# A two-branch attention kernel: the hand-built interleaving of its jobs replaced by a list scheduler with modelled engine times

## The chip, the cores and the metric

The kernel runs on one core of one Trainium2 chip. The metric is device time in microseconds (us) of one execution. The kernel before takes 1214.83 us (median of 3 runs, 1211.84 to 1217.28). A core has five engines that each work through their own instruction stream in order: PE (TensorE: matmuls, results go to PSUM), ACT (ScalarE), DVE (VectorE), POOL (GpSimd) and SP (which issues transfers). They wait for one another by semaphores. Both kernels share out eight PSUM tiles of 128 x 512 fp32, called banks below.

## The reference, cut to what matters

```python
x = A_x                                             # 1 x 2048 x 512, bf16
g = sigmoid((x * gate_w).sum(-1, keepdims=True))
# A: full attention, 32 heads of 16
qkv = (x @ A_wqkv) ...
p = softmax(einsum("bhqd,bhkd->bhqk", q, k) * 16 ** -0.5)
a = einsum("bhqk,bhkd->bhqd", p, v) ... @ A_wo
# B: each position looks at 8 earlier ones, 2 apart (same sizes, own weights)
...
return g * a + (1 - g) * b
```

The heavy part is A's exponentials. Scores are made transposed, in tiles of 128 keys x 512 queries of one head: 4 query chunks x 32 heads x 16 key blocks = 2048 tiles. A *period* is one query chunk of four heads: 64 tiles, and there are 32 periods. B runs beside it, mostly on POOL.

## The kernel before

Each tile needs one score matmul (32 rows of the array, 128 columns), one exponential, and one accumulating matmul (128 rows, 17 columns). Most tiles are exponentiated on ACT in sets of three or two, out of two PSUM rings (3 + 2 banks). Exactly six tiles of each period go to DVE instead, which does exp with four operations. One bank is the accumulator, one (`misc`) serves all projections and output jobs, one (`wv`) the DVE exps.

```python
CFG = dict(dve_units=6, burst_budget=2, fill_min=1, pv_lag=2, ...)

def misc_ps(shape, dtype=FP32, tag="misc"):          # ONE bank for all side jobs
    return ps.tile(shape, dtype, tag=tag, bufs=1, name="misc_ps")

def emit_junk():                                     # filler: result never read
    jt = misc_ps([128, QW])
    mm_ct(jt, ident[:], ones_t[:], True, True)       # four matmuls, 128 rows x 32 columns each

def emit_dve(k, u_):                                 # a tile for DVE
    wv = ps.tile([128, QW], FP32, tag="wv", bufs=1, name="wv")
    mm(wv[:], kt_all[...], qt_tiles[(c_, i)][...], True, True, ...)
    dve_ops.extend([ ... four lambdas: ta, ta, ta, pd ... ])

for k in range(nsets + LAG):                         # one step = one exp set
    flush_deadline(k)                                # jobs whose step has come
    ...
    if even:
        emit_qk(k, False)                            # score matmuls + the ACT exp
        cost = pop_misc(k, budget, only_continue=True)
        emit_pv(k - LAG)                             # accumulate set k-2
        cost += pop_misc(k, budget - cost)           # a budget of side work
        if cost < cfg["fill_min"] and k < nsets:
            emit_junk()
    ...
    pop_bg(k, 1)
    pop_dve(2)                                       # two DVE operations per step
```

So the order on every engine is set by counting exp sets, with budgets and deadlines in sets; no engine's time is known to it.

## Time and profile before

| | before |
|---|---|
| time | 1214.83 us |
| ACT busy / PE busy / DVE busy | 877 / 911 / 828 us of 1213.8 |
| exp tiles on ACT / DVE | 1856 / 192 |
| first exp starts at | 30.4 us |
| ACT waits for score matmuls | 277 us |
| mean clock granted to PE | 0.89 |

The page of the kernel before; the rows of digits are busy tenths in 40 equal slices of the span, PEclk is PE's clock in tenths of full speed:

```profile
span 1213.8 us, 22328 instructions
...
PE 911.3 (75%) x9313; PEld 279.6 (23%) x9313; DVE 827.5 (68%) x1306; ACT 877.3 (72%) x763; POOL 590.5 (49%) x540
...
PE   5877677877847676887777787777777877777775
...
ACT  1766666766847677878777777777788878797874
...
PEclk9898998988879888879898988788799998898898
```

No engine is full, and the clock is often not. The costliest groups (count | busy us, mean ns of one | idle us before them and what ended it): ACT's exps, the filler on PE, and the first of the four DVE operations of an exp tile.

```profile
L107 ACT ACTIVATE pT<-ring 128x1536 bf16<-128x1536 f32 x743 | 868.4, 1246 | 301.4 <-PE ring L116 277.2
...
L116 PE MATMUL misc_ps<-ones_t,ident 128*32 128x512 bf16 x1360 | 209.2, 422 | 13.1 <-DVE qt L107 10.1
...
L107 DVE TENSOR_SCALAR ta<-wv 128x512 f32<-128x512 uint16 x192 | 131.4, 684 | 89.8 <-PE wv L116 87.5
```

The waits (total us, times, longest us). ACT, the engine with most work that cannot be avoided, waits 277 us for PE; PE waits 112 us for DVE to free the only `wv` bank:

```profile
engine line waited for: us in total, times, longest us
...
ACT pT L107 <- PE ring L116: 277.2, 190, 14.0
...
PE wv L116 <- DVE pd L107: 111.5, 72, 4.2
```

Between stops ACT is fed well. In this piece of PE's timeline (start, duration) the score matmuls of a set of three start at 608.87 and again at 611.14: five tiles in 2.27 us, ACT's own pace.

```profile
608.87 0.39 PE L116 MATMUL ring<-qt,kt_all 32*128 32x512 bf16 x3 [0.42 <-ACT pT L107]
...
609.20 0.39 PE L116 MATMUL acc<-pT,vp_all 128*17 128x512 bf16 x2
...
610.39 0.39 PE L116 MATMUL ring<-qt,kt_all 32*128 32x512 bf16 x2
611.14 0.39 PE L116 MATMUL ring<-qt,kt_all 32*128 32x512 bf16 x3 [0.36 <-ACT pT L107]
```

The stop itself, as PE's timeline has it, idle time in brackets:

```profile
769.87 0.58 PE L116 MATMUL wv<-qt,kt_all 32*128 32x512 bf16 x1 [3.78 <-DVE pd L107]
```

And windows of 2.5 us around it (busy us and instructions of PE, PE's weight loads, DVE, ACT, POOL; then the clock):

```profile
core 0: us, PE busy (x) PEld busy (x) DVE busy (x) ACT busy (x) POOL busy (x), PEclk, DMA share, GB/s
765.00:767.50 2.50, 1.09 (x16) 0.17 (x9) 2.46 (x3) 1.93 (x3) 2.36 (x2) 1.00 0.00 0
767.50:770.00 2.50, 0.13 (x1) 0.00 (x0) 2.21 (x4) 0.84 (x1) 2.33 (x4) 0.66 0.00 0
770.00:772.50 2.50, 2.50 (x18) 0.67 (x19) 1.94 (x3) 0.00 (x0) 2.50 (x3) 0.50 0.00 0
772.50:775.00 2.50, 2.33 (x16) 0.32 (x11) 1.76 (x4) 2.10 (x2) 2.50 (x3) 0.50 0.30 69
775.00:777.50 2.50, 2.44 (x19) 0.52 (x20) 1.80 (x3) 1.09 (x2) 2.34 (x3) 0.50 1.07 343
777.50:780.00 2.50, 2.50 (x35) 0.73 (x25) 0.58 (x1) 1.74 (x3) 2.50 (x3) 0.80 0.96 331
```

From about 766.1 to 769.9 PE does nothing: it stands at a `wv` matmul until DVE is through. The clock falls within that stop and is 0.50 for some ten microseconds, and ACT starves meanwhile. Such a stop comes about once per period: in the whole trace PE stands idle for over 2 us 28 times, start included, and there are 32 periods.

### The profile page before, as it was taken

How to read it: one execution, taken by the hardware profiler on the slowest of the kernel's cores; microseconds unless marked ns; L12 is line 12 of the kernel's file. 1: busy time of each engine (PE TensorE's matmuls, PEld its weight loads, DVE VectorE, ACT ScalarE, POOL GpSimd, SP SyncE). 2: the span in 40 equal slices, each digit the busy share in tenths (PEclk: the TensorE clock that was granted, in tenths of full speed). 3: DMA queues.
4: the chain of work that ended last, by engine and by line, in shares of the span. 5: the costliest groups of instructions: out<-in, count | busy, mean ns of one | idle time of the engine just before them, and what ended most of it. 6: DMA issues, size and time to landing. Idle time of an engine off the chain costs nothing.

```text
span 1213.8 us, 22328 instructions
## 1 busy us (share of the span) xinstructions
PE 911.3 (75%) x9313; PEld 279.6 (23%) x9313; DVE 827.5 (68%) x1306; ACT 877.3 (72%) x763; POOL 590.5 (49%) x540
## 2 busy tenths in 40 slices
PE   5877677877847676887777787777777877777775
PEld 3323221322212121212122222122222222122221
DVE  4866887787637676667666767666767677766665
ACT  1766666766847677878777777777788878797874
POOL 2014564719193748293929292929475656500000
PEclk9898998988879888879898988788799998898898
DMA  6011102003001132020200202202020021000000
GB/s 206 14 36 49 40 1 87 24 24 119 1 1 40 49 105 70 1 70 1 70 1 1 92 23 79 70 1 70 1 70 1 15 75 35 1 1 1 1 2 18
DMA packets 44397, 47.61 MB, mean 39 GB/s; under 512 B 2260, under 2 KB 41732, under 8 KB 44296
## 3 DMA queue, kind: packets, MB, share of 16 engines
q1 hardware_dynamic: 44296, 46.19, 12.0%
q8 instruction: 72, 1.18, 0.4%
q14 instruction: 29, 0.24, 0.1%
HBM read 39.86 MB, written 6.33 MB: 38 GB/s over the span
## 4 chain that ended last, share of the span: by engine, by line
DVE 41%; PE 31%; ACT 16%; issue 9%; POOL 2%; DMA 0%; ACTq 0%; POOLq 0%; DVEq 0%
DVE ta L107 17%; ACT pT L107 15%; PE misc_ps L116 14%; PE ring L116 7%; PE acc L116 7%; DVE pd L107 5%; PE wv L116 3%; DVE ott L107 2%; DVE qt L107 2%; POOL prod L107 2%; DVE kt_all L107 2%; DVE oat L107 2%; DVE accT L107 2%; DVE kmax_all L107 1%; DVE absq L107 1%
## 5 line engine op out<-in xcount | busy, mean ns | idle before, releaser
L107 ACT ACTIVATE pT<-ring 128x1536 bf16<-128x1536 f32 x743 | 868.4, 1246 | 301.4 <-PE ring L116 277.2
L116 PE MATMUL acc<-pT,vp_all 128*17 128x512 bf16 x1856 | 354.7, 418 | 10.6 <-ACT pT L107 9.9
L116 PE MATMUL ring<-qt,kt_all 32*128 32x512 bf16 x1856 | 293.2, 416 | 54.2 <-ACT pT L107 51.8
L107 POOL TENSOR_TENSOR prod<-vsh,attn 128x512 f32<-128x512 bf16 x128 | 140.0, 1125 | 348.2 <-issue 164.8
L107 DVE SCALAR_TENSOR_TENSOR ta<-ta,wv 128x512 f32<-128x512 f32 x384 | 263.1, 685 | 11.5
L107 POOL TENSOR_TENSOR prod<-prod 128x512 f32<-128x512 f32 x192 | 223.8, 1180 | 5.0
L116 PE MATMUL misc_ps<-ones_t,ident 128*32 128x512 bf16 x1360 | 209.2, 422 | 13.1 <-DVE qt L107 10.1
L107 POOL TENSOR_TENSOR prod<-ksh,qb 128x512 f32<-128x512 bf16 x128 | 146.4, 1175 | 103.9 <-DVE qb L107 96.9
L107 DVE TENSOR_SCALAR ta<-wv 128x512 f32<-128x512 uint16 x192 | 131.4, 684 | 89.8 <-PE wv L116 87.5
L116 PE MATMUL wv<-qt,kt_all 32*128 32x512 bf16 x192 | 81.3, 424 | 111.5 <-DVE pd L107 111.5
L116 PEld LDWEIGHTS <-vp_all 128*17 128x17 bf16 x2048 | 95.6, 92 | 285.1 <-issue 256.2
L107 DVE SCALAR_TENSOR_TENSOR pd<-ta,wv 128x512 uint16<-128x512 f32 x192 | 131.9, 687 | 7.1
L116 PEld LDWEIGHTS <-kt_all 32*128 32x128 bf16 x2048 | 64.6, 92 | 311.2 <-issue 308.9
L116 PE MATMUL misc_ps<-xT,wst 128*16 128x512 bf16 x1024 | 96.2, 437 | 5.2 <-ACT xT L107 3.1
L116 PE MATMUL acc<-pd,vp_all 128*17 128x512 bf16 x192 | 81.6, 425 | 0.6 <-DVE pd L107 0.6
L107 DVE STREAM_TRANSPOSE accT<-acc 128x512 f32<-128x512 f32 x32 | 22.8, 712 | 77.1 <-PE acc L116 77.1
L116 PE MATMUL misc_ps<-bw,xT 128*32 128x512 bf16 x768 | 66.8, 410 | 5.6 <-DVE kvs L107 3.3
L116 PEld LDWEIGHTS <-ident 128*32 128x32 bf16 x1360 | 55.6, 96 | 53.7 <-issue 46.2
L116 PE MATMUL misc_ps<-woarr,oat 128*32 128x512 bf16 x512 | 48.4, 435 | 7.6 <-DVE oat L107 2.6
L116 PEld LDWEIGHTS <-xT 128*32 128x32 bf16 (+1 forms) x1088 | 38.4, 99 | 43.3 <-issue 35.3
L107 DVE CAST kvs<-misc_ps 128x512 bf16<-128x512 f32 x32 | 22.1, 689 | 35.1 <-PE misc_ps L116 35.1
L116 PEld LDWEIGHTS <-wst 128*16 128x16 bf16 x1024 | 32.0, 95 | 49.7 <-issue 37.6
(79 smaller groups left out, 580.3 us busy)
## 6 DMA issues: line engine op xcount, KB each, us to landing
ksh<-kv_scr SPq DMA_DIRECT2D x16, 1024.0 KB, 8.7
vsh<-kv_scr SPq DMA_DIRECT2D x16, 1024.0 KB, 6.3
kv_scr<-kvs SPq DMA_DIRECT2D x16, 256.0 KB, 2.1
out_dram<-osb SPq DMA_DIRECT2D x16, 128.0 KB, 1.7
wst<-in_A_wqkv_dram SPq DMA_DIRECT2D x3, 512.0 KB
bw<-in_B_wqkv_dram SPq DMA_DIRECT2D x1, 1536.0 KB
xld<-in_A_x_dram SPq DMA_DIRECT2D x2, 512.0 KB, 5.7
xld_70<-in_A_x_dram SPq DMA_DIRECT2D x1, 512.0 KB, 7.1
```

Source lines behind the costliest of these rows:

```text
L107: return chain_on(key, f(*a, **k))
L116: return chain(nc.tensor.matmul(out, lhsT=lhsT, rhs=rhs, start=start, stop=stop, **kw))
```

## The change

Nearly everything is rewritten. Each job (a projection, an exp set, a DVE exp, a B block, ...) becomes a generator that yields steps with an engine, a priority and a modelled duration, and takes and gives back buffers by name. A small list scheduler runs all jobs in modelled time while the program is built; the order in which it starts steps becomes the order on each engine. The two single-purpose PSUM banks become one pool of two slots, `w`. Two streams take tiles for DVE whenever a slot is free that no other job wants. The core of the diff:

```diff
-def misc_ps(shape, dtype=FP32, tag="misc"): ...        # and "wv" for DVE exps
-def emit_junk(): ...
-for k in range(nsets + LAG): ...
+class Plan:
+    LAT = 0.08
+    def run(self):
+        while True:
+            # engine step or buffer request that can start earliest in modelled time
+            ...
+            x = min((y for y in lst if y[2] <= st + 1e-9), key=lambda y: (y[0], y[1]))   # priority
+            x[5]()                                      # emits the instructions
+            self.free[nm] = st + x[4]                   # modelled duration
+            self.advance(x[3], st + x[4] + self.LAT, None)
+P.resource("w", 2)
+P.resource("rA", 1); P.resource("rB", 1); ...
+MM = 0.29; VP = 0.66; EXP_PRIO = 60
+
+def act_stream():
+    ...
+        def f():
+            for s_, (p_, t, j) in enumerate(units):
+                qk_mm(ring[:, s_, :], p_, t, j)
+        yield ("pe", 0, MM - 0.06 + 0.03 * len(units), f)
+        yield ("spawn", act_tail(...))                  # ACT: 0.074 + 0.4267 * n
+
+def dve_stream(z):
+    while ...:
+        s = yield ("acq", "w", EXP_PRIO)                # last in line for a slot
+        u = dve_pick(t_now)
+        ...
+        yield ("pe", 1.5, MM - 0.03, lambda: qk_mm(wv_[:], p, t, j))
+        yield ("dve", pr, VP - 0.05, ...)               # four times
+        yield ("rel", "w", s)
...
-chain(nc.tensor.transpose(out=pxt[...], in_=xl[...], identity=ident[:]))   # x transposed on PE
+SP.dma_start_transpose(out=xT[:, :, sc * QW:(sc + 1) * QW], in_=x2d[...])  # x transposed by the load
-mm_init(pk, e32, QW)                                     # constants by matmul
+V.tensor_scalar(out=kt, in0=pk[:], scalar1=kbias[:, 0:1], ...)             # constants as a bias
```

The Q job and the step after the accumulator also lose DVE operations, and A's output projection loses half its matmuls.

## The prediction

> **What bounds the kernel now.** No engine is full: the busy table gives ACT 877 us (72%), PE 911 (75%), DVE 828 (68%) of 1213.8. The groups show 1856 score tiles exponentiated on ACT and 192 on DVE (four operations of 0.685 us each). Where ACT runs undisturbed (timeline, 606 to 615 us) five tiles take 2.26 us, so 1856 need 839 us. First exp starts at 30.4 us, the last accumulation ends at about 1203.5: 1173 us for 839 us of ACT work. The waits name the loss: ACT waits 277 us for PE's score matmuls, up to 14 us at a time; PE waits 112 us for DVE to free the one PSUM tile of the DVE exps. After such a stop the clock falls: windows of 2.5 us show PE busy 0.13 us at 767.5 to 770, then clock 0.50 until about 779, and five tiles then cost about 3 us. The Trainium skill, "TensorE: Matmul & The Clock Gate" (Part 1), describes this halving after an idle window; the trace agrees (mean 0.89). So the limit is in-order engines stopping one another about once per period (32 periods), not throughput.
>
> **What the change does.**
> - Ordering: a fixed order from modelled times, two PSUM slots shared by all side jobs and two DVE exp streams. This attacks the stops.
> - PE: removes filler matmuls (1360 in 340 groups of 0.22 to 0.25 us, 75 to 85 us), initialising matmuls of K and Q (96 groups, about 21 us), half of A's output projection; adds transposes after the accumulator. I sum PE's real need to about 800 us (845 now, filler included).
> - DVE without exps: 301 us now (828 less 526), about 245 after: Q drops from 2.2 to 1.4 us a period, the post step from 2.65 to about 1.75.
> - DVE exps: independent operations start 0.61 us apart in the timeline (601.56, 602.17), dependent ones 0.72, so two interleaved streams need about 2.5 us a tile instead of 2.74 plus waits. DVE filled to 93% does some 240 tiles instead of 192; ACT then needs (2048-240)x0.452 = 817 us.
> - POOL's chain is the same (590 us) and off the path.
>
> **Sum.** Start 28, tail 9 (10 now), ACT 817 us, now 71% efficient. All three engines then need 800 to 830 us, so they will collide, and the order is right only as far as the modelled times are; I expect ACT 86 to 90% busy between start and tail: 817/0.885 = 923, plus 37: 960 us, 21% less.
>
> **Predicted: 960 us, range 890 to 1060.** Faster by over 2%: 0.94; within 2%: 0.03; slower: 0.03.
>
> **What would show each step.** About 720 ACT exps; about 960 DVE exp operations, DVE busy over 82%; ACT's wait for score matmuls down from 277 to under 120 us, longest under 6; PE's wait on DVE exps from 112 to under 40; mean clock at least 0.94; the remaining loss spread over many short waits, no longer one per period. First exp at 25 to 33 us.
>
> **What would make it wrong.** The clock: with the filler gone PE may fall to half speed more often, and PE's 800 us become the bound (over 1050). The order: if a DVE operation or PE group takes longer than modelled (exp operations modelled 0.61, dependent ones measured 0.72), every later instruction waits in order and the stops return. The transposing loads of x, whose duration no trace here shows, may delay the start by 10 to 20 us. The other way: if plan and chip agree closely, about 890.

## The result, and the profile after

The changed kernel takes 986.31 us (median of 3 runs, 985.65 to 990.4), correct; the ratio to before is 0.813 (95% interval 0.8085 to 0.8174). Ratios here and below are the mean time of one kernel's fast runs over that of the other's of the same rounds, so not quite the ratio of the medians quoted.

| | before | predicted | after |
|---|---|---|---|
| time, us | 1214.83 | 960 (890 to 1060) | 986.31 |
| first exp, us | 30.4 | 25 to 33 | 36.5 |
| exp tiles on ACT / DVE | 1856 / 192 | 1808 / 240 | 1879 / 169 |
| DVE busy | 68% | over 82% | 69% |
| ACT waits for score matmuls, us | 277 | under 120 | 75.8 |
| mean clock | 0.89 | at least 0.94 | 0.84 |

The page after, the same lines:

```profile
span 983.9 us, 18122 instructions
...
PE 892.3 (91%) x7296; PEld 270.9 (28%) x7296; DVE 677.5 (69%) x1178; ACT 871.6 (89%) x770; POOL 583.6 (59%) x543
...
PE   2899999999999988998999989989989989899986
...
ACT  0489999999899998998989998898999988998894
...
PEclk8679999999799997798759777796799885976795
```

ACT is busy 89% of the span, and so is PE at 91%. But the clock row is worse than before, mostly in its second half. The groups show 169 tiles on DVE:

```profile
L191 ACT ACTIVATE pT<-ring 128x1536 bf16<-128x1536 f32 x752 | 867.2, 1275 | 86.4 <-PE ring L191 75.8
...
L191 PE MATMUL acc<-pd,vp_all 128*17 128x512 bf16 x169 | 75.2, 479 | 6.2 <-DVE pd L191 5.4
```

The waits: ACT's wait for PE is down from 277 to 76 us, and 22.6 of that is the start. The wait for DVE that stopped PE for 112 us is gone; 5.4 us remain at the accumulating matmuls, and 2.1 us at the slots (summed over `w_...`, whose tiles this kernel names one by one, so that the view splits them).

```profile
engine line waited for: us in total, times, longest us
...
ACT pT L191 <- PE ring L191: 75.8, 81, 22.6
...
PE acc L191 <- DVE pd L191: 5.4, 15, 0.9
```

Now windows of 2.5 us in the second half (columns as before):

```profile
577.50:580.00 2.50, 1.87 (x14) 0.49 (x13) 2.46 (x5) 2.50 (x3) 2.50 (x3) 1.00 0.03 7
580.00:582.50 2.50, 2.18 (x14) 0.54 (x12) 2.32 (x5) 2.50 (x3) 2.34 (x3) 1.00 0.00 0
582.50:585.00 2.50, 1.61 (x11) 0.46 (x10) 2.50 (x5) 2.50 (x4) 2.50 (x3) 0.88 0.00 0
585.00:587.50 2.50, 2.50 (x12) 0.44 (x11) 1.73 (x3) 1.44 (x3) 2.50 (x4) 0.50 0.02 6
587.50:590.00 2.50, 2.50 (x16) 0.53 (x13) 1.90 (x4) 2.50 (x3) 2.42 (x2) 0.50 0.95 310
590.00:592.50 2.50, 2.50 (x13) 0.34 (x11) 2.46 (x4) 1.95 (x3) 2.34 (x3) 0.50 0.32 107
```

PE never stops for long here (its longest idle time from 577.5 to 585 is 0.63 us), and yet the clock goes to 0.50 at about 584.4 and stays there while PE is busy all of every window. In the stop shown before the change, the half clock followed an idle PE. This is another thing. The timeline at the same place (start, duration, instruction, idle before it):

```profile
584.81 0.58 PE L191 MATMUL acc<-pd,vp_all 128*17 128x512 bf16 x1 [0.27 <-DVE pd L191]
...
585.32 0.60 PE L191 MATMUL w_8005<-qt,kt_all 32*128 32x512 bf16 x1
...
585.86 0.60 PE L191 MATMUL acc<-pd,vp_all 128*17 128x512 bf16 x1
...
586.38 0.61 PE L191 MATMUL ring<-qt,kt_all 32*128 32x512 bf16 x3
...
586.92 0.60 PE L191 MATMUL acc<-pT,vp_all 128*17 128x512 bf16 x3
587.10 4.62 ACT L191 ACTIVATE pT<-ring 128x1536 bf16<-128x1536 f32 x4 [1.06 <-PE ring L191]
...
588.60 0.61 PE L191 MATMUL ring<-qt,kt_all 32*128 32x512 bf16 x3
```

Each PE group now lasts 0.51 to 0.54 us to the next (0.33 us at full clock, as at 608.87 to 609.20 above). Three groups from 584.81 to 586.38 serve DVE tiles alone; in that time no set for ACT is made, and ACT's exp at 587.10 has waited 1.06 us.

How the 984 us of the profiled run split: 36.5 us to the first exp; 935.3 us to the end of the last exp (971.8), for 1879 tiles that need 1879 x 0.452 = 849 us of ACT at the pace of five per 2.26 us, so 91% efficient; 12.1 us of tail. The prediction had 28 + 817/0.885 + 9.

### The profile page after: what moved, and what is told of

The parts are those of the page before. It is cut to its first block, busy times and chain, and to the rows that moved or that the text cites. A ratio compares the mean times of both kernels' runs of the same rounds, so it can differ in the third digit from the quotient of the medians.

```text
span 983.9 us, 18122 instructions
## 1 busy us (share of the span) xinstructions
PE 892.3 (91%) x7296; PEld 270.9 (28%) x7296; DVE 677.5 (69%) x1178; ACT 871.6 (89%) x770; POOL 583.6 (59%) x543
## 4 chain that ended last, share of the span: by engine, by line
PE 48%; ACT 24%; DVE 14%; issue 10%; DMA 2%; SPq 0%; ACTq 0%; DVEq 0%
ACT pT L191 24%; PE acc L191 18%; PE ring L191 14%; DVE ta L191 9%; DVE pd L191 3%; DMA xT<-in_A_x_dram 2%; DVE accS L191 1%; ACT lg L191 0%; DVE kt_all L191 0%; DVE lg L191 0%; DVE qt L191 0%; DVE absq L191 0%; PE w_5455 L191 0%; PE w_11876 L191 0%; PE w_6192 L191 0%
## 5 line engine op out<-in xcount | busy, mean ns | idle before, releaser
L191 ACT ACTIVATE pT<-ring 128x1536 bf16<-128x1536 f32 x752 | 867.2, 1275 | 86.4 <-PE ring L191 75.8
L191 PE MATMUL ring<-qt,kt_all 32*128 32x512 bf16 x1879 | 353.4, 436 | 49.2 <-ACT pT L191 43.4
L191 PE MATMUL acc<-pT,vp_all 128*17 128x512 bf16 x1879 | 336.3, 432 | 0.0
L191 POOL TENSOR_TENSOR prod<-prod 128x512 f32<-128x512 f32 (+1 forms) x208 | 240.5, 1170 | 6.3
L191 POOL TENSOR_TENSOR prod<-vsh,lg 128x512 f32<-128x512 bf16 x128 | 136.6, 1098 | 117.7 <-issue 114.9
L191 PEld LDWEIGHTS <-kt_all 32*128 32x128 bf16 x2048 | 102.7, 93 | 354.8 <-issue 343.6
L191 PEld LDWEIGHTS <-vp_all 128*17 128x17 bf16 x2048 | 72.4, 89 | 220.9 <-issue 219.4
L191 DVE COPY accS<-acc 128x512 f32<-128x512 f32 x32 | 22.0, 688 | 14.5 <-PE acc L191 13.7
L191 DVE TENSOR_REDUCE kmax_all<-kt_all 128x1 f32<-128x512 bf16 x32 | 21.8, 684 | 0.9
L191 POOL TENSOR_TENSOR ob<-prod 128x512 f32<-128x512 f32 x16 | 20.3, 1270 | 1.3
L191 POOL TENSOR_TENSOR obb<-ob,prod 128x512 bf16<-128x512 f32 x16 | 20.3, 1270 | 1.3
```

The lines of the kernel that those rows point to most:

```text
L191: return chain_on(self._key, f(*a, **k))
```

## The experiments

Twelve kernels ran, all correct. The questions: does the low clock cost anything, and what does the clock follow? What is a DVE tile worth? How much comes from the order, from the pooled slots, and from the work saved? And where did the start go?

**Theory A** says that the removed filler had kept the clock up, and that the stretches with only score and accumulating matmuls now run at half clock and pay for it. **Rival B** says that filler is ballast and the clock only mirrors waits.

### 1. Filler put back, and its controls

The filler accumulates zeros into the open accumulator, so it needs no bank and waits for nobody; one group whenever two exp sets passed without a projection on PE (label `after_fill`).

```diff
 def f():
+    since[0] += 1                       # mm_ct (every projection) sets it to 0
+    if since[0] >= 2:
+        filler()                        # 272 groups in all
     for s_, (p_, t, j) in enumerate(units):
         qk_mm(ring[:, s_, :], p_, t, j)
+def filler():
+    acc = acc_tiles[open_[-1]]; since[0] = 0
+    for c4 in range(4):
+        mm(acc[32 * c4:32 * c4 + 32], z32[:], ones_t[:], False, False, tile_position=(0, 32 * c4))
```

> The changed kernel with 272 groups of four full-height (128-row) matmuls with zero weights put back, one before the score matmuls whenever two exp sets passed with no projection on PE. Theory A (the half clock in stretches of only score and accumulate matmuls is what the removed filler cost): mean clock from 0.84 to 0.95 or more, time from 986 to 925-960 us although PE has 272 x 0.22 = 60 us more to do. Rival B (filler is ballast, the clock only follows waits): clock stays near 0.84, time 1000-1040 us.

Measured: 957.58 us, ratio 0.788 (0.7857 to 0.7904), clock 0.961. The page:

```profile
PE 870.4 (92%) x8384; PEld 276.7 (29%) x8384; DVE 673.0 (71%) x1178; ACT 873.3 (92%) x770; POOL 584.8 (62%) x543
...
PEclk8799999999999999998999999898999999999985
```

More work on PE, less time, and PE is even busy for less time (870 us against 892), since every group is shorter at full clock. Nor is it PE's short idle times: in the windows from 577.5 to 585 us PE is busy 2.30, 2.06 and 1.53 us with the filler (1.87, 2.18 and 1.61 without), and the clock stays at 1.00. Theory A holds, rival B falls.

The first control (`after_fill_narrow`) keeps number, place and length of the filler but uses a corner of the array:

```diff
-        mm(acc[32 * c4:32 * c4 + 32], z32[:], ones_t[:], ...)
+        mm(acc[32 * c4:32 * c4 + 1], z32[0:32, 0:1], ones_t[0:32, :], ...)
```

> The same 272 groups at the same places and of the same length (512 columns), but each matmul uses 32 rows and one column of the array instead of 128 rows and 32 columns. If the clock follows how much of the array works (A1): clock stays near 0.84 and time is 990-1040 us. If it follows PE being busy at all (A2): same as after_fill, 925-960 us.

Measured: 1044, 1047 and 1063 us in three runs, which count as slow, and 1017.8 in the fastest; clock of the profiled run, a slow one, 0.837, and of the fastest 0.872. Even that one is slower than the change without any filler (986.3, clock 0.84).

```profile
PE 983.6 (94%) x8384; PEld 284.5 (27%) x8384; DVE 675.6 (65%) x1178; ACT 883.4 (85%) x770; POOL 584.2 (56%) x543
...
PEclk8789999989899998888859997958658987865765
```

In this run PE is busy 94% and the clock is still low, so being busy does not by itself keep it up. (The profiled run is one of the slow ones; that the narrow filler does not help is read from the fastest run's time and clock as well.) The next (`after_fill_rows`) changes one thing against it, all 128 rows but still one column:

```diff
-        mm(acc[32 * c4:32 * c4 + 1], z32[0:32, 0:1], ones_t[0:32, :], ...)
+        mm(acc[32 * c4:32 * c4 + 1], z32[:, 0:1], ones_t[:], ...)
```

> after_fill with filler matmuls of all 128 rows but one column of the array each (four of 128 columns used) instead of 32 each. If the clock follows the rows that the moving data passes (or its bytes), it stays at 0.95 and the time at 950-960 us. If it follows the cells that work (rows times columns), it behaves as after_fill_narrow: clock under 0.87, 1010-1050 us.

Measured: 962.29 us, ratio 0.7904 (0.7858 to 0.795), clock 0.957, the same as with 32 columns.

```profile
PE 871.3 (91%) x8384; PEld 273.9 (29%) x8384; DVE 673.1 (71%) x1178; ACT 873.0 (92%) x770; POOL 585.2 (61%) x543
...
PEclk8699999999999999898999999899999998999985
```

These last two kernels differ only in 32 or 128 rows of moving data. So between these fillers the clock went with the rows that data passes through, not with the columns that were in use, and not with whether PE was busy. Fast runs alone part the two kernels: 1017.8 us at clock 0.872 with 32 rows, 954 to 965 us at 0.944 to 0.961 with all. (The filler's weights are zeros; that sufficed.) What it is about the rows stays open: with them the bytes of moving data and the part of the array that four matmuls side by side cover change too. Nor are 128 rows enough as such: the accumulating matmuls have 128 rows as well, and the clock fell in stretches of those and score matmuls.

The dose:

```diff
-    if since[0] >= 2:
+    if since[0] >= 1:                   # 659 groups
```

> The dose: 659 filler groups, one before every set of score matmuls, instead of 272. Theory A: the clock is already 0.96, so only cost is left: about 390 x 0.22 = 85 us more PE work, part of it in PE's gaps: 965-1010 us. If the clock was still what bounds after_fill: under 950 us.

Measured: 1004.68 us, ratio 0.8257 (0.8218 to 0.8297), clock 0.982. The clock was bought already; the extra 387 groups only cost (PE is busy 945 of 1004 us).

And the same question to the kernel before:

```diff
-    fill_min=1,
+    fill_min=0,
```

> The kernel before with its 340 filler groups switched off, nothing else. Theory A: mean clock from 0.89 to about 0.7-0.8, time from 1215 to 1250-1350 us. Rival B, and the rival that the gain of the change came from less PE work: 1150-1215 us, since 75 to 85 us of PE work are gone.

Measured: 1233.86 us, ratio 1.0154 (1.0117 to 1.0191), clock 0.77. The filler was worth keeping there too, but theory A expected at least 35 us and it is 20. Nor did less work on PE gain anything by itself: 1360 matmuls fewer made that kernel no faster (its clock fell with them).

### 2. What DVE's tiles are worth, and what that has to do with the clock

```diff
-    for z in range(2):
+    for z in range(0):
         P.spawn(dve_stream(z))
```

> The changed kernel with no exp tile on DVE (169 move to ACT). By ACT's rate 169 x 0.452 = 76 us more than 986: 1062 us, if each DVE tile is worth its full ACT time. If the half clock makes DVE tiles dear (each needs two more narrow PE groups of 0.54 us at half clock, 169 x 1.08 = 182 us of PE), most of that is given back and it is 1000-1035 us.

> The same with the filler (321 groups by the same rule). If the filler helps mainly because it keeps DVE tiles cheap on PE, it gains under 15 us over after_nodve, since five tiles on ACT alone need only 4 x 0.54 = 2.16 us of PE at half clock against 2.26 us of ACT: 1000-1020 us, and the DVE tiles are then worth 45-65 us with a full clock. If the filler helps whatever DVE does, it gains 25-35 us here too.

Measured medians (clock of the profiled run; the left and the right column come from different calls, whose medians of the kernel before agree to about 0.1%):

| | 169 tiles on DVE | none on DVE |
|---|---|---|
| no filler | 986.3 (0.84) | 1033.5 (0.78) |
| filler | 957.6 (0.96) | 1031.4 (0.90) |

This shows when the low clock costs. Without DVE tiles the clock is 0.78, and lifting it to 0.90 gains 2 us, within the spread of the runs: ACT itself is the limit there (busy 942 of the 985 us from its first exp to its last without the filler, 950 of 980 with it). An estimate says why: five tiles that all go to ACT need four PE groups; at half clock that is 4 x 0.54 = 2.16 us, still under ACT's 2.26. A DVE tile whose matmuls stand alone adds two groups: 1.08 us of PE at half clock, which does not fit. So a slow PE eats the help that DVE gives: 169 tiles spare ACT 169 x 0.452 = 76 us, and are worth 47 us without the filler and 74 us with it. (Expected with the filler were 1000 to 1020 us and 45 to 65 us for the tiles, both missed; the gain of under 15 us came true.)

### 3. The order or the pooled slots

```diff
-    P.resource("w", 2)
+    P.resource("w", 1)                  # side jobs
+    P.resource("wd", 1)                 # DVE exps, one stream
```

To avoid deadlocks the Q job here waits for its selector before it takes the slot, and the gate job gets priority 5 instead of 20.

> The changed kernel with the two PSUM slots divided as in the kernel before: one for the side jobs, one for a single DVE exp stream (the Q job waits for its selector before it takes the slot, and the gate job gets an earlier priority, to avoid a deadlock). If the gain of the change comes from the modelled order alone, the time stays within 40 us of 986. If it comes mostly from pooling the slots, it goes to 1080 us or more. I expect between: 1030-1060 us.

Measured: 1035.02 us, ratio 0.8525 (0.8492 to 0.8559), clock 0.873. With the banks divided as before, the rewrite keeps 179 of its 229 us; the pool, with the second stream that it allows, gives the last 49. It is not a matter of how many tiles DVE takes: here it takes 190 (busy 738 us), against 169 (678 us) with the pool, and the time is longer. The new wait is at the bank of the one DVE stream, where DVE now waits for PE (before the change that wait was 87.5 us):

```profile
DVE ta L191 <- PE wv L191: 123.2, 119, 3.9
```

### 4. Work saved, or a plan that fits

Both kernels are the one with filler, plus 96 reductions of 0.68 us on DVE, 65 us in all, after the accumulator's step. They emit the same kind and number of extra instructions. In one the plan counts them, in the other it does not, and only that differs in the source. The plan then differs in more than the order: it gives DVE 156 tiles when it counts them and 169 when it does not.

```diff
 yield ("dve", 3, 0.45, nrm)
+for _ in range(3):                                            # planned
+    yield ("dve", 3, VP, lambda: V.tensor_reduce(out=dum[:], in_=st["s"][:], ...))
```
```diff
-yield ("dve", 3, 0.45, nrm)
+yield ("dve", 3, 0.45, nrm_more)     # unplanned: nrm and the three reductions, as 0.45 us
```

> after_fill with 96 more DVE reductions of 0.69 us (three per period, 66 us in all, results unused), which the plan knows of. If the DVE work that the change saved (about 56 us by my sum) is a large part of its gain, the time rises by 40 us or more, to about 1000. If DVE has room (it is busy 71%), the plan only gives it some tiles fewer (156 instead of 169, worth 13 x 0.45 = 6 us): 960-970 us.

> The same 96 reductions, but the plan counts them as taking no time, so the order is made for a DVE that is 2.1 us per period faster than it is. If the order must fit the real times closely, the stops return: 980 us or more. If the slots and waits have enough slack, it is within 10 us of the planned one.

Measured: planned 957.88 us, ratio 0.7898 (0.784 to 0.7957); unplanned 1009.69 us, ratio 0.8284 (0.8233 to 0.8335), with one run of 1037.65 outside its fast runs. The waits of ACT, planned and then unplanned:

```profile
ACT pT L191 <- PE ring L191: 41.8, 55, 21.8
```

```profile
ACT pT L191 <- PE ring L191: 84.3, 99, 22.1
```

The DVE work that the change saves (about 56 us by the prediction's sum) is no part of the gain by itself: 65 us put back cost nothing, against 957.58 for the kernel without them (the plan gives DVE fewer tiles for it: DVE is busy 694 us, 21 more than without). The same work, unknown to the plan, costs 52 us, with ACT's wait for PE doubled and the clock down from 0.973 to 0.924; how the 52 us divide between the stops and the clock was not tested. Here more work was absorbed, and an order made for other times was not.

### 5. The start, and the best version

After the change the first exp came later, not earlier. SP holds 23 us to issue four transposing loads, one after the other, and PE waits for what they bring; moreover its clock is 0.50 from about 17.8 to 41.7 us, having fallen in an idle stretch of 7.2 us.

```profile
0.74 23.05 SPq L191 DMA_TRANSPOSE xT<-in_A_x_dram  x4
```

```diff
-A.dma_start(out=bw[:], ...)  # also bwo, awo
+SP.dma_start(out=bw[:], ...) # behind the loads of x
 # Q job of period 0:
+yield ("wait", ev_k[0][2])   # before it takes a slot
 # plan: x arrives at 11 us, then every 5 us; 57 filler groups in PE's waits before the first scores
```

> after_fill with the start changed: the three weight loads that are not needed at once go behind the loads of x, the first Q job takes its PSUM slot only after the third K job, the plan's arrival times of x are set to 11 us plus 5 us each, and 57 filler groups stand in PE's waits before the first score matmuls. First exp from about 35 us to 27-31 us, and the time from 958 to 948-954 us. If the start is hidden behind other work: no change, within 3 us of 958.

Measured: 948.04 us, ratio 0.7804 (0.7769 to 0.784); first exp at 27.7 us, against 34.5 in the kernel with filler alone. The same four loads now hold SP for 15 us, and the clock is 1.00 from 0 to 45 us:

```profile
0.74 15.05 SPq L194 DMA_TRANSPOSE xT<-in_A_x_dram  x4
```

So the 23 us were not the loads' own: in the kernel whose weight loads stand behind them they took a third less. Which of the four edits gave how much was not separated. Then the dose once more, `since[0] >= 3`:

> after_fill_start with a filler group only after three exp sets without a projection instead of two: 133 groups instead of 272. If the clock stays at 0.93 or more, PE has 30 us less to do: 938-947 us. If the smaller dose lets the clock fall (below 0.93), 950-965 us.

Measured: 939.0 us, ratio 0.7712 (0.767 to 0.7753), clock 0.957 to 0.968 in the three fast runs. The profiled run, at 948.82 us (clock 0.945), was over 1.5% above the fastest and counts as slow; the ratio rests on the fast ones. This is the best version: 5% under the change as given.

## Why the prediction was right or wrong

The time (960, measured 986) lay in the range, and the stops that it named are gone. Three of its terms were wrong, and a fourth, a guess, came out a little better than expected and made up for part of them; that the sum came so close is in part luck.

- **"The limit is in-order engines stopping one another about once per period"**: right. ACT's wait for score matmuls fell from 277 to 75.8 us; after the start (from 40 us on) the longest is 2.6 us where it had been 14. PE's 112 us on DVE's exps are gone. Experiment 4 shows that the saved DVE work does not do it and that an order made for the wrong times undoes 52 us of it; by experiment 3 pooled banks with the second stream are 49 us of it.
- **"DVE filled to 93% does some 240 tiles"**: this step failed. It is 169, fewer than before, with DVE busy 69%. The prediction took DVE's time for the limit; the runs point to PSUM. A DVE tile holds one of two slots through four operations, and its stream is last in line. From 500 to 550 us, where projections and output jobs hold the slots, the DVE operations on `ta` number 13, and from 550 to 600, 56 (busy us, count, clock, DMA share, GB/s; four operations make a tile). In experiment 3, with a bank of its own, a single stream took 190 tiles:

```profile
500.00:550.00 50.00, 7.47 (x13) 0.87 0.24 73
550.00:600.00 50.00, 35.47 (x56) 0.67 0.26 85
```

  The term is 169 x 0.452 = 76 us spared on ACT, not 108, so ACT needs 849 us, not 817: 32 us.
- **"Mean clock at least 0.94"**: failed, 0.84. The prediction read the clock from idle windows only. It named the removed filler as a risk, but thought that then PE would be the bound at over 1050 us. The runs put the cost at 29 us (986.3 to 957.6, the filler's own work included), and experiment 2 finds it only where DVE takes tiles, which need PE groups of their own.
- **"First exp at 25 to 33 us"**: failed, 36.5. The transposing loads were named as a risk of 10 to 20 us; it was 8.5 against the 28 in the sum, at half clock from 17.8 us on. Experiment 5 brought the first exp from 34.5 to 27.7 us and the time down by 9.5.
- **"ACT 86 to 90% busy between start and tail"**: 91% by the same measure (849 of 935 us), slightly better in spite of the lower clock. This, which no step of the prediction explains, balanced part of the errors above (at the foreseen 0.885 the 849 us of work would have taken 959 us, 24 more).

Left open: the first step of the gain, 1214 to 1035 us, mixes the order with the rewritten jobs; no experiment takes the old jobs through the new order, and the matmuls saved in A's output projection and in initialising were not put back. Whether more DVE tiles would help could not be tried: giving their streams an earlier turn for the slots made programs that deadlock while they are built (as the kernel of experiment 3 did at first, where three periods' accumulators came to need two buffers that the plan does not know of); that is not shown here. The narrow filler was worse than none in part by its plain cost (PE is busy 984 us against 892, in a slow run); why its runs are so uneven is not explained. How few full-height matmuls keep the clock up was not found: 133 groups (with the new start) gave 0.957 to 0.968 in fast runs, hardly less than the 0.961 to 0.972 of 272.

## What to carry to other kernels

When no engine is full, look for which in-order engine stops which, and give the order to something that knows durations; then check those durations, since 65 us of work known to the plan cost nothing and the same work unknown to it cost 52. Before removing work that looks like ballast, look at the clock beside it: here full-height filler made the kernel 29 us faster, and 2 us without the tiles on DVE, which make PE scarce. And count banks before counting an engine's free time: DVE had time left for more tiles, and few came where other jobs held the PSUM slots.

## What the Trainium skill lacked or had wrong

- "TensorE: Matmul & The Clock Gate", Part 1, has the clock gate follow how busy PE is. It warns of idle gaps, long ones and frequent short ones alike. The halving after an idle stretch agrees: before the change PE stood still for 3.78 us up to 769.87 us, and by the mean of the window from 767.5 to 770 (0.66) the clock fell some 2.2 us into it (an estimate). But the runs also show clock 0.50 with PE busy 2.50 of 2.50 us in every window shown from 585 us on, and at much the same idle times beforehand the kernel with filler kept 1.00. Filler of 32 rows left the clock at 0.872 (its one fast run), filler of 128 rows raised it to 0.957 (one column) and 0.961 (32 columns): between these fillers what counted was rows. The page does not say so.
- The same page has no figure for how much such work is enough: in fast runs 133 groups gave 0.957 to 0.968 and 272 gave 0.961 to 0.972 (both with the new start), 272 gave 0.954 to 0.970 and 659 gave 0.982 to 0.994 (both without it), and the time was best with the fewest.
- "TensorEngine Tiling (Array Packing)", Key Properties, says that changing the tiling mode drains the engine. The trace is in line with it (at full clock a score group is followed by an accumulating group after 0.33 us, 608.87 to 609.20, and that by another of the same mode after 0.21 us, 609.20 to 609.41), but the page gives no cost, and none at half clock, where the step is 0.51 to 0.54 us. A DVE tile that stands alone pays two such steps on PE.
- No page that I found says how long a transposing load of this size holds the queue that issues it on this chip: 23.05 us for four of 512 KB on SP, about 5.8 us each, and 15.05 us, about 3.8 each, with the three weight loads issued after them instead of beside them.
